# Joining the attention blocks of three chunk pairs on TensorE: Y and S with the next pair's A

## The chip, the cores and the metric

The kernel runs on one core of one Trainium2 chip. The metric is the device time of one execution in microseconds (us); lower is better.

## The reference

Retention with a decaying state, then a feed-forward layer with the activation h * cos(h). Shapes: q, k, v are (4, 8, 768, 64); w_in is 512 x 2048, w_out 2048 x 512; everything is float32.

```python
for t in range(S):                                   # attention, per batch and head
    state = gamma * state + outer(k[t], v[t])
    y[t] = scale * q[t] @ state
h = x @ w_in                                         # x: y as (3072, 512)
out = (h * np.cos(h)) @ w_out
```

## The kernel before

The sequence is cut into chunks of 128 steps. One "pair" p is one chunk of two batches; there are 12 pairs (0 to 11). For each pair TensorE does three small jobs beside the large feed-forward matmuls:

- A: scores, k times q. The contraction is only 64 deep, so two heads run at once in the upper and lower 64 rows of the array (64x128 tiling).
- Y: the outputs, from the masked scores and from the state. Each result is 64 columns wide, so two heads run at once in the left and right half (128x64 tiling).
- S: the update of the state, also in 128x64 tiling.

Each of these jobs writes its results into banks. A bank is one of the program's seven 128x512 PSUM tiles, and it is free again when another engine has read it; the state has a tile of its own. Between A and Y, VectorE masks the scores (`stage_m`). After S it copies the state to SBUF. Y is cast by ScalarE into `xt`, the input of the feed-forward units.

```python
def stage_a(p, b):                       # A: 8 matmuls, row tiling
    ...
    for a in range(HP):
        for j in range(2):
            po = 64 * j
            nc.tensor.matmul(ap[j][:, a, :], lhsT=kt(n, b, a)[po : po + 64, :],
                             rhs=qt(n, b, a)[po : po + 64, :], tile_position=(po, 0))

def half_y(p, b):                        # Y: 16 matmuls, column tiling
    ...
            nc.tensor.matmul(yp[ts(j, 64), a, :], lhsT=stb[p % 2][:, b, a, ts(j, 64)],
                             rhs=qt(n, b, a), start=True, stop=False, ...)
            ...
            nc.tensor.matmul(yp[ts(j, 64), a, :], lhsT=vs[n][:, b, 2 * a + j, :],
                             rhs=am[p % 2][b][j][:, a, :], ...)
    nc.scalar.copy(out=xt[...], in_=yp)

def stage_s(p, copy_st):                 # S: 16 matmuls, column tiling, then the state copy
    ...
                    nc.tensor.matmul(st_ps[ts(j, 64), b, a, :], lhsT=qk[n][:, b, 1, h, :],
                                     rhs=vs[n][:, b, h, :], ...)
    for j in range(2):
        copy_st(out=stb[(p + 1) % 2][...], in_=st_ps[ts(j, 64)])
```

From the third group of pairs on, a loop spreads this over "units". A unit is one feed-forward quarter (`unit_f`, four 128x128 by 128x512 matmuls) and mostly one output quarter (`unit_o`, four more). A of a pair stands at unit 2 of its eight, Y and S (`later`) at unit 6:

```python
for g in range(2, NG + 1):
    for s in range(16):
        hf, r = divmod(s, 8)
        p = 2 * (g + 1) + hf
        ...
            unit_f(g, s)
        ...
                unit_o(g - 1, *divmod(s, 4))
        if p < NP:
            if r == 0:
                ahead(p + 1)             # conversions on GpSimd and ScalarE
            elif r == 1:
                stage_t_dma(p + 1)       # transposes of q and k by DMA
            elif r == 2:
                todo = [stage_a(p, b) for b in range(2)]
                stage_m(p, todo[0])
            elif r == 3:
                stage_m(p, todo[1])
            elif r == 6:
                later(p)                 # Y, S, then the loads of a pair behind
```

Of the kernel before, what the change touches and what calls it, by code (L numbers as in the profile page):

```python
# [47 lines left out]
def kernel(  # L48
# [9 lines left out]
    nc = tc.nc  # L58
    B, H, S, D = q.shape
    C = 128  # L60
    NC = S // C
# [22 lines left out]
    clk = Clock()  # L84
# [42 lines left out]
    def load(eng, p, names):  # L127
        bp, c = divmod(p, NC)
        for n in names:
            t, src = SRC[n[0]]  # L130
            b = int(n[1])
            eng.dma_start(  # L132
                out=t[SLOT[p]][b],
                in_=src[2 * bp + b, :, ds(c * C, C)].rearrange("h t d -> t h d"))
# [65 lines left out]
    def conv_v(p, eng, bs=(0, 1)):  # L200
        for b in bs:
            eng.tensor_tensor(out=vs[p % NB][:, b], in0=vf[SLOT[p]][b],  # L202
                              in1=bc(gk, p % NC), op=ALU.mult)
# [33 lines left out]
    def stage_t_dma(p):  # L237
        n = p % NB
        for b in range(2):
            nc.sync.dma_start_transpose(  # L240
                out=qkt[n][:, b].rearrange("p w a t -> p (w a) t"),
                in_=qk[n][:, b].rearrange("p w h d -> p (w h d)"))
# [7 lines left out]
    def stage_a(p, b):  # L250
        n = p % NB
        bk = [banks.take(), banks.take()]
        ap = [t.rearrange("p (a t) -> p a t", a=HP) for t in bk]
# [4 lines that stand above are left out]
                                 rhs=qt(n, b, a)[po : po + 64, :],  # L258
                                 tile_position=(po, 0))
        clk.run("pe", 0.3)  # L260
        return b, bk, ap, clk.pe

    def stage_m(p, item, parts=(0, 1)):
        b, bk, ap, done = item
        for j in parts:
            nc.vector.tensor_tensor(  # L266
                out=am[p % 2][b][j], in0=ap[j],
                in1=mask.unsqueeze(1).to_broadcast([128, HP, 128]), op=ALU.mult)
            banks.give(bk[j], clk.run("dve", 0.64, done + 0.1))
# [22 lines left out]
    def stage_s(p, copy_st):  # L292
        c = p % NC
        n = p % NB
        if c == NC - 1:
            return
        for b in range(2):
            for a in range(HP):
                for j in range(2):
                    h = 2 * a + j  # L300
                    nc.tensor.matmul(  # L301
                        st_ps[ts(j, 64), b, a, :], lhsT=qk[n][:, b, 1, h, :],
                        rhs=vs[n][:, b, h, :], start=(c == 0 and b == 0 and a == 0),
                        stop=True, skip_group_check=True)
        for j in range(2):
            copy_st(out=stb[(p + 1) % 2][ts(j, 64), :, :, ts(j, 64)], in_=st_ps[ts(j, 64)])  # L306
            clk.run("act" if copy_st == nc.scalar.copy else "dve", 0.65, clk.pe + 0.3)
        clk.run("pe", 0.25)

    def stage_y(p, copy_st=nc.vector.tensor_copy):  # L310
        for b in range(2):
            half_y(p, b)
        stage_s(p, copy_st)
# [15 lines left out]
    def unit_f(g, f):  # L329
        bank = banks.take()  # L330
        for i in range(KIN):
            nc.tensor.matmul(bank, lhsT=w_in_t(i, f), rhs=xt[g % 2][:, i, :],  # L332
                             start=(i == 0), stop=(i == KIN - 1))
        banks.give(bank, act(bank, gt[g % 2][:, f, :]))
# [33 lines left out]
    def unit_o(g, j, part):  # L368
        if part == 0:
            o_bank[j] = banks.take()  # L370
        bank = o_bank[j]
        for f in range(4 * part, 4 * part + 4):
            nc.tensor.matmul(bank, lhsT=gt[g % 2][:, f, ts(j, 128)], rhs=w_out_sb[:, f, :],  # L373
                             start=(f == 0), stop=(f == KOUT - 1))
        clk.run("pe", 0.87)
        if part == 3:
            o = ob[j % 4]
            bp, c = divmod(2 * g + j // 2, NC)
            dst = out[ds((2 * bp + j % 2) * S + c * C, C), :]
            nc.scalar.copy(out=o, in_=bank)  # L380
            nc.sync.dma_start(out=dst, in_=o)
            banks.give(bank, clk.run("act", 0.6, clk.pe + 0.1))

    def last_o(g, j):
        bp, c = divmod(2 * g + j // 2, NC)
        dst = out[ds((2 * bp + j % 2) * S + c * C, C), :]
        for i, (a, n) in enumerate(((0, 320), (320, 192))):
            bank = banks.take()
            for f in range(KOUT):
                nc.tensor.matmul(bank[:, :n], lhsT=gt[g % 2][:, f, ts(j, 128)],  # L390
                                 rhs=w_out_sb[:, f, ds(a, n)],
                                 start=(f == 0), stop=(f == KOUT - 1))
            o = ob[i]
            if i:
                nc.vector.tensor_copy(out=o[:, :n], in_=bank[:, :n])
                nc.scalar.dma_start(out=dst[:, ds(a, n)], in_=o[:, :n])
            else:
                nc.scalar.copy(out=o[:, :n], in_=bank[:, :n])
                nc.sync.dma_start(out=dst[:, ds(a, n)], in_=o[:, :n])
# [61 lines left out]
    clk.run("pe", 0.0, 12.4)  # L461
    stage_m(1, stage_a(1, 1))
    stage_s(0, nc.scalar.copy)
    half_y(0, 1)
    warm(3)
    half_y(1, 0)
    banks.give(spare, clk.pe)
    half_y(1, 1)
    stage_s(1, nc.scalar.copy)
    first_f()  # L470
    for f in range(4, 16):
# [53 lines left out]
    def ahead(p):  # L525
        if p < NP:
            conv_q(p, nc.gpsimd)
            conv_k(p, True)
            conv_v(p, nc.gpsimd)

    def later(p):
        stage_y(p)
        n = 8 if p == 4 else p + 3 if p > 5 else NP
        if n < NP:
            load(nc.gpsimd, n, ("q0", "k0", "q1", "k1", "v0", "v1"))

    def o_units(g, a, b):
        for u in range(a, b):
# [4 lines left out]
    stage_t_dma(6)  # L543
    o_units(1, 2, 6)
    later(4)
    attend(5)
    o_units(1, 6, 10)
    later(5)
# [5 lines that stand above are left out]
            if g == 2 and s % 2 == 0 and s < 12:  # L554
                unit_o(1, *divmod(10 + s // 2, 4))
            if g < NG:
                unit_f(g, s)
            if g > 2:
                if g < NG or s < 12:
                    unit_o(g - 1, *divmod(s, 4))  # L560
                elif s == 12:
                    last_o(g - 1, 3)
            if p < NP:
                if r == 0:
                    ahead(p + 1)
                elif r == 1:
                    if p + 1 < NP:
                        stage_t_dma(p + 1)
                elif r == 2:
                    todo = [stage_a(p, b) for b in range(2)]  # L570
                    stage_m(p, todo[0])
                elif r == 3:
                    stage_m(p, todo[1])
                elif r == 6:
                    later(p)


# [28 lines left out]
```

## Time and profile before

| | before |
|---|---|
| time, median of 6 runs | 209.66 us (209.38 to 210.15) |
| span of the profile | 208.1 us |
| PE busy | 201.2 us, 97% |
| granted TensorE clock (share of full speed) | 0.998 |

The first part of the page gives busy time, share of the span and count of instructions for each engine:

```profile
PE 201.2 (97%) x1646; PEld 113.0 (54%) x1646; DVE 112.8 (54%) x188; ACT 114.3 (55%) x193; POOL 102.3 (49%) x118
```

The chain that ended last, as shares of the span by engine:

```profile
PE 92%; DMA 3%; DVE 2%; issue 1%; SPq 0%; ACT 0%; DVEq 0%
```

The list of waits of PE (engine, line, what it waited for, total us, times, longest):

```profile
PE bank L407 <- DVE gt L172: 1.2, 1, 1.2
PE bank L257 <- DVE qkt L214: 1.1, 2, 0.6
PE bank L230 <- DVE qk L195: 0.9, 1, 0.9
```

The kernel is bound by TensorE, and all three waits lie in the start-up. After it, TensorE waits for no one. A change on another engine can therefore gain nothing after the start-up; only TensorE's own stream can get shorter. Where is that stream not dense? The timeline of PE shows it (columns: start us, duration us, engine, line, operation, out<-in, shapes, count). First the lone A block of pair 9, then the lone Y and S block of the same pair:

```profile
119.95 1.03 PE L373 MATMUL bank<-w_out_sb,gt 128*128 128x512 bf16 x4
120.91 0.62 PE L257 MATMUL bank<-qkt 64*128 64x128 bf16 x16
121.46 1.05 PE L332 MATMUL bank<-xt,w_in 128*128 128x512 bf16 x4
...
127.53 1.03 PE L373 MATMUL bank<-w_out_sb,gt 128*128 128x512 bf16 x4
128.49 0.25 PE L279 MATMUL bank<-qkt,stb 128*64 128x128 bf16 x2
...
129.40 0.42 PE L301 MATMUL st_ps<-vs,qk 128*64 128x64 bf16 x16
129.75 1.05 PE L332 MATMUL bank<-xt,w_in 128*128 128x512 bf16 x4
```

Ends of matmuls are modelled, so read the starts only. In the dense stream a 128x512 matmul starts every 216 ns, so the four from 119.95 use the array until 120.81. A starts at 120.91, 0.10 us late. Its 16 matmuls start in twos, every 56 ns: until 121.36. The next dense one starts at 121.46, again 0.10 us late. It is the same on entering Y (128.39 and 128.49) and on leaving S. In the single records the second step after an edge is longer by another 10 to 28 ns. I call such a change between 128x128, 64x128 and 128x64 an edge; each costs 0.10 to 0.13 us.

Not every change of operands is an edge. The transposes on TensorE in the same trace use other weights, another bank and only 128 columns, but the whole array:

```profile
36.77 1.03 PE L373 MATMUL bank<-w_out_sb,gt 128*128 128x512 bf16 x4
37.63 1.06 PE L230 MATMUL bank<-ident,qk 128*128 128x128 bf16 x16
38.52 0.81 PE L373 MATMUL bank<-w_out_sb,gt 128*128 128x512 bf16 x3
```

Four times 216 ns after 36.77 is 37.63, and 16 times 56 ns later is 38.52: nothing is lost on either side.

The loads of weights show what an edge is made of. These two lines are of PEld, one at an edge, one in the dense stream:

```profile
120.90 0.45 PEld L257 LDWEIGHTS <-qkt 64*128 64x128 bf16 x16 [0.42 <-issue]
...
122.14 0.74 PEld L373 LDWEIGHTS <-gt 128*128 128x128 bf16 x4
122.35 1.03 PE L373 MATMUL bank<-w_out_sb,gt 128*128 128x512 bf16 x4
```

In the dense stream the weights are loaded 0.21 us ahead of their matmul (122.14 for 122.35), during the matmul in front. At the edge they are loaded only when A begins (120.90 for 120.91). The Trainium skill, "TensorE: Matmul & The Clock Gate", Part 2, says that TensorE pulls weight loads ahead of matmuls in flight when the row groups do not conflict or the load goes to the background weight buffer. This trace agrees in the dense stream, where the load leads by 0.21 us; at the edges it leads by 1 to 5 ns only. That the pipeline has to empty there is what the skill's "TensorEngine Tiling (Array Packing)", Key Properties, states; the trace shows the gap, not the emptying itself.

### The profile page before, as it was taken

How to read it: one execution, taken by the hardware profiler on the slowest of the kernel's cores; microseconds unless marked ns; L12 is line 12 of the kernel's file. 1: busy time of each engine (PE TensorE's matmuls, PEld its weight loads, DVE VectorE, ACT ScalarE, POOL GpSimd, SP SyncE). 2: the span in 40 equal slices, each digit the busy share in tenths (PEclk: the TensorE clock that was granted, in tenths of full speed). 3: DMA queues.
4: the chain of work that ended last, by engine and by line, in shares of the span. 5: the costliest groups of instructions: out<-in, count | busy, mean ns of one | idle time of the engine just before them, and what ended most of it. 6: DMA issues, size and time to landing. Idle time of an engine off the chain costs nothing.

```text
span 208.1 us, 4181 instructions
## 1 busy us (share of the span) xinstructions
PE 201.2 (97%) x1646; PEld 113.0 (54%) x1646; DVE 112.8 (54%) x188; ACT 114.3 (55%) x193; POOL 102.3 (49%) x118
## 2 busy tenths in 40 slices
PE   7789999999999999999999999999999999999993
PEld 3257554558897555546545445445445444444452
DVE  4691984544957454869874574574575234443000
ACT  6677873157996336577654744744534653553120
POOL 8999238389999999999999200000000000000000
PEclk9999999999999999999999999999999999999999
DMA  6999999999999999979895231141101101110212
GB/s 161 345 240 200 215 251 290 330 247 306 277 221 276 297 211 303 236 217 225 259 226 193 76 80 49 61 97 50 50 3 50 50 9 45 50 52 16 85 74 81
DMA packets 36644, 33.83 MB, mean 163 GB/s; under 512 B 26768, under 2 KB 29072, under 8 KB 36624
## 3 DMA queue, kind: packets, MB, share of 16 engines
q0 software_dynamic: 7808, 20.98, 37.6%
q1 hardware_dynamic: 28672, 12.49, 24.0%
q8 instruction: 13, 0.21, 0.4%
q10 hardware_dynamic: 144, 0.10, 0.1%
q14 instruction: 7, 0.06, 0.1%
HBM read 27.26 MB, written 6.29 MB: 161 GB/s over the span
## 4 chain that ended last, share of the span: by engine, by line
PE 92%; DMA 3%; DVE 2%; issue 1%; SPq 0%; ACT 0%; DVEq 0%
PE bank L373 38%; PE bank L332 32%; PE bank L343 7%; PE bank L257 3%; DMA qf<-in_q_dram 3%; PE bank L279 3%; PE bank L284 3%; PE bank L390 2%; PE st_ps L301 1%; DVE am L266 1%; PE bank L354 1%; PE bank L230 1%; PE bank L361 1%; DVE qkt L214 1%; SPq L132 0%
## 5 line engine op out<-in xcount | busy, mean ns | idle before, releaser
L325 DVE TENSOR_TENSOR gt<-bank,cosb 128x512 bf16<-128x512 f32 x96 | 64.9, 689 | 63.5 <-ACT cosb L321 63.3
L321 ACT ACTIVATE cosb<-bank,halfpi 128x512 bf16<-128x512 f32 x96 | 65.1, 688 | 50.3 <-PE bank L332 45.9
L373 PE MATMUL bank<-w_out_sb,gt 128*128 128x512 bf16 x368 | 89.6, 379 | 0.0
L332 PE MATMUL bank<-xt,w_in 128*128 128x512 bf16 x304 | 75.4, 380 | 0.0
L373 PEld LDWEIGHTS <-gt 128*128 128x128 bf16 x368 | 35.5, 98 | 41.3
L332 PEld LDWEIGHTS <-w_in 128*128 128x128 bf16 x304 | 33.5, 114 | 30.3
L266 DVE TENSOR_TENSOR am<-bank,mask 128x512 bf16<-128x512 f32 x48 | 30.4, 682 | 1.1 <-PE bank L257 1.1
L380 ACT COPY ob<-bank 128x512 f32<-128x512 f32 x23 | 13.4, 586 | 17.9 <-PE bank L373 17.9
L132 POOL DMA_DIRECT2D vf<-in_v_dram x23 | 20.2, 884 | 5.3 <-DMA w_out_sb<-in_moe_w_out_dram 5.3
L202 POOL TENSOR_TENSOR vs<-vf,gk 128x512 bf16<-128x512 f32 x21 | 21.4, 1040 | 0.4 <-PE st_ps L301 0.3
L195 POOL TENSOR_TENSOR qk<-qf,gq 128x512 bf16<-128x512 f32 x18 | 18.6, 1058 | 2.9 <-DMA qf<-in_q_dram 2.8
L132 POOL DMA_DIRECT2D kf<-in_k_dram x21 | 18.9, 900 | 1.8 <-DMA w_out_sb<-in_moe_w_out_dram 1.6
L208 ACT CAST qk<-kf 128x512 bf16<-128x512 f32 x24 | 13.9, 615 | 9.3 <-DMA kf<-in_k_dram 9.2
L288 ACT CAST xt<-bank 128x512 bf16<-128x512 f32 x24 | 13.0, 587 | 7.9 <-PE bank L284 7.7
L132 POOL DMA_DIRECT2D qf<-in_q_dram x18 | 16.2, 901 | 0.8 <-DMA w_in<-in_moe_w_in_dram 0.8
L343 PE MATMUL bank<-xt,w_in 128*128 128x256 bf16 x128 | 14.7, 273 | 0.0
L343 PEld LDWEIGHTS <-w_in 128*128 128x128 bf16 x128 | 13.8, 114 | 0.4
L284 PE MATMUL bank<-am,vs 128*64 128x128 bf16 x192 | 11.7, 220 | 0.0
L279 PEld LDWEIGHTS <-stb 128*64 128x64 bf16 x160 | 8.8, 109 | 4.3 <-issue 3.1
L306 DVE CAST stb<-st_ps 64x512 bf16<-64x512 f32 x12 | 8.2, 687 | 4.9 <-PE st_ps L301 4.7
L279 PE MATMUL bank<-qkt,stb 128*64 128x128 bf16 x160 | 10.7, 222 | 0.1
L284 PEld LDWEIGHTS <-vs 128*64 128x64 bf16 x192 | 10.0, 110 | 0.5 <-issue 0.4
(46 smaller groups left out, 86.2 us busy)
## 6 DMA issues: line engine op xcount, KB each, us to landing
vf<-in_v_dram POOLq DMA_DIRECT2D x23, 256.0 KB, 5.9
out_dram<-ob SPq DMA_DIRECT2D x23, 256.0 KB, 2.0
kf<-in_k_dram POOLq DMA_DIRECT2D x21, 256.0 KB, 5.9
qf<-in_q_dram POOLq DMA_DIRECT2D x18, 256.0 KB, 5.6
w_out_sb<-in_moe_w_out_dram POOLq DMA_DIRECT2D x4, 512.0 KB, 12.9
qf<-in_q_dram SPq DMA_DIRECT2D x6, 256.0 KB, 7.8
w_in<-in_moe_w_in_dram POOLq DMA_DIRECT2D x3, 512.0 KB, 8.1
kf<-in_k_dram POOLq DMA_DIRECT2D x1, 512.0 KB, 6.1
```

The source lines that it names most:

```text
L132: eng.dma_start(out=t[SLOT[p]][b], in_=src[2 * bp + b, :, ds(c * C, C)].rearrange("h t d -> t h d"))
L195: eng.tensor_tensor(out=qk[p % NB][:, b, 0], in0=qf[SLOT[p]][b], in1=bc(gq, p % NC), op=ALU.mult)
L202: eng.tensor_tensor(out=vs[p % NB][:, b], in0=vf[SLOT[p]][b], in1=bc(gk, p % NC), op=ALU.mult)
L208: nc.scalar.copy(out=qk[p % NB][:, b, 1], in_=kf[SLOT[p]][b])
L266: nc.vector.tensor_tensor(out=am[p % 2][b][j], in0=ap[j], in1=mask.unsqueeze(1).to_broadcast([128, HP, 128]), op=ALU.mult)
L279: nc.tensor.matmul(yp[ts(j, 64), a, :], lhsT=stb[p % 2][:, b, a, ts(j, 64)], rhs=qt(n, b, a), start=True, stop=False, skip_group_check=True)
L284: nc.tensor.matmul(yp[ts(j, 64), a, :], lhsT=vs[n][:, b, 2 * a + j, :], rhs=am[p % 2][b][j][:, a, :], start=(c == 0), stop=True, skip_grou ...
L321: nc.scalar.activation(out=cb, in_=bank, func=AF.Sin, bias=halfpi)
L325: nc.vector.tensor_tensor(out=out, in0=bank, in1=cb, op=ALU.mult)
L332: nc.tensor.matmul(bank, lhsT=w_in_t(i, f), rhs=xt[g % 2][:, i, :], start=(i == 0), stop=(i == KIN - 1))
L343: nc.tensor.matmul(bank[:, ts(e, 256)], lhsT=w_in_t(i, f + e), rhs=xt[g % 2][:, i, ts(hf, 256)], start=(i == 0 and e == 0), stop=(i == KIN ...
L373: nc.tensor.matmul(bank, lhsT=gt[g % 2][:, f, ts(j, 128)], rhs=w_out_sb[:, f, :], start=(f == 0), stop=(f == KOUT - 1))
```

## The change

Y and S of pairs 8, 9 and 10 are placed in the same block as A of the pair behind (9, 10, 11). Two lone blocks have four edges (in and out of each); a joined one has three (in, S to A, out). To let A follow S directly, the state copy of S is put off by two units, behind the masks. The last pair's loads stand two units sooner in the program. Its core:

```diff
+    def state_out(p, copy_st):            # the state copy, taken out of stage_s
+        ...
+    joined = {(3, 10): 8, (3, 14): 9, (4, 10): 10}
+
+    def join(p, now):
+        stage_y(p, None)
+        todo = [stage_a(p + 1, b) for b in range(2)]
+        stage_m(p + 1, todo[0])
+        put_off(now + 1, lambda: stage_m(p + 1, todo[1]))
+        put_off(now + 2, lambda: state_out(p, nc.vector.tensor_copy))
 ...
-                elif r == 2:
+                elif r == 2 and p in (6, 7, 8):
                     todo = [stage_a(p, b) for b in range(2)]
 ...
-                elif r == 6:
+                elif r == 6 and p in (6, 7, 11):
                     later(p)
+                elif (g, s) == (3, 4):
+                    fetch(11)
+                if (g, s) in joined:
+                    join(joined[g, s], 16 * g + s)
```

More of the change, by code (lines that the diff above doesn't have):

```diff
@@ L304, in stage_s @@
                         stop=True, skip_group_check=True)
+        clk.run("pe", 0.25)
+        if copy_st is not None:
+            state_out(p, copy_st)
+    def state_out(p, copy_st):
+        if p % NC == NC - 1:
+            return
         for j in range(2):
             copy_st(out=stb[(p + 1) % 2][ts(j, 64), :, :, ts(j, 64)], in_=st_ps[ts(j, 64)])
-            clk.run("act" if copy_st == nc.scalar.copy else "dve", 0.65, clk.pe + 0.3)
-        clk.run("pe", 0.25)
+            clk.run("act" if copy_st == nc.scalar.copy else "dve", 0.65, clk.pe + 0.1)
     def stage_y(p, copy_st=nc.vector.tensor_copy):
@@ L529, in ahead, with fetch @@
             conv_v(p, nc.gpsimd)
+    def fetch(p):
+        load(nc.gpsimd, p, ("q0", "k0", "q1", "k1", "v0", "v1"))
     def later(p):
@@ L534, in later, with put_off @@
         if n < NP:
-            load(nc.gpsimd, n, ("q0", "k0", "q1", "k1", "v0", "v1"))
+            fetch(n)
+    late = []
+    def put_off(when, step):
+        late.append((when, step))
+    joined = {(3, 10): 8, (3, 14): 9, (4, 10): 10}
[5 more added lines that the diff above has]
+        put_off(now + 2, lambda: state_out(p, nc.vector.tensor_copy))
     def o_units(g, a, b):
@@ L562 @@
                     last_o(g - 1, 3)
+            while late and late[0][0] <= 16 * g + s:
+                late.pop(0)[1]()
             if p < NP:
@@ L568 @@
                         stage_t_dma(p + 1)
-                elif r == 2:
+                elif r == 2 and p in (6, 7, 8):
                     todo = [stage_a(p, b) for b in range(2)]
                     stage_m(p, todo[0])
-                elif r == 3:
-                    stage_m(p, todo[1])
-                elif r == 6:
+                    put_off(16 * g + s + 1, lambda todo=todo, p=p: stage_m(p, todo[1]))
+                elif r == 6 and p in (6, 7, 11):
                     later(p)
+                elif (g, s) == (3, 4):
+                    fetch(11)
+                if (g, s) in joined:
+                    join(joined[g, s], 16 * g + s)
 _INS = ['q', 'k', 'v', 'moe_w_in', 'moe_w_out']
```

## The prediction

> **What bounds the kernel now.** TensorE. The page has PE busy 97% of the 208.1 us span, and the chain of waits puts 92% of the span on PE. The list of waits shows only three PE waits over the run, all in the start-up, and none after 20 us: From there on the 128x512 matmuls start every 216 ns. What is not dense is the edges of the attention blocks. Reading single start times (timeline of PE and PEld around 120.6 and 128.2 us):
>
> - last dense matmul to first of A: 311 ns for 216, then 63 for 56: about 105 ns for entering A;
> - last of A to first dense: 149 ns for about 53, then 242 for 216: about 122 ns for leaving;
> - entering Y: 309 for 216, then 76 for 56: about 115 ns; leaving S: 128 for about 29, then 242 for 216: about 125 ns.
>
> The Trainium skill, "TensorEngine Tiling (Array Packing)", Key Properties, says that changing the tiling mode drains the TensorE. These gaps agree: dense is 128x128, A is 64x128, Y and S are 128x64.
>
> **What the change removes, adds and moves.** TensorE's instructions are the same in number; only the order differs. For pairs 8, 9 and 10 the Y/S block and the A block of the next pair become one, so there is one edge fewer each time: leaving S (125) and entering A (105) are gone, and a direct S-to-A edge is added. The kernel before already has such a joined block once, at 70.4 to 72.7 us: S to A there is 128 ns for 29, then 62 for 56, about 105 ns. So one join saves about 125 ns. From sums: a lone Y/S block costs 1.387 us over dense matmuls, a lone A block 0.675; the joined one 1.94. Three joins: about 0.37 us.
>
> The state copy moves two units later on VectorE (2 x 0.70 us), behind the first-half and second-half masks (2 x 0.64 us each). The earlier loads change nothing: the order of instructions on GpSimd, SyncE is the same in both kernels, and GpSimd runs ahead of TensorE (done at 116 us).
>
> **On the critical path.** All of the 0.37 us, if no new wait arises. Candidates, estimated from the trace's durations:
> - one of A's banks belongs to the feed-forward unit just before. Its multiply ends 2.5 us after that unit begins; A's second half begins 3.4 us after.
> - Y of the next pair, four units (some 7 us) after the join, needs masks and state: done about 1 us before.
> - pair 10's transposes are issued at 118 to 120.6 us and land in 2.7 to 7.6 us; A now needs them at about 130.
>
> **Predicted time.** 209.74 - 0.37 = 209.37 us; the runs differ by 0.4 among themselves. Range 208.95 to 209.95. Faster by over 2%: 0.01; within 2%: 0.98; slower by over 2%: 0.01.
>
> **What would show it right or wrong.** Right: span near 207.7 us; lone groups near 113, 137 and 144 us gone, joined ones near 121, 129 and 153 with S to A in 128 ns; no PE wait in the list of waits after 20 us; other starts keep 216 ns. VectorE's state copies at about 2 units after S, its total unchanged.
>
> **What would make it wrong.** A PE wait on VectorE in a join (bank still held by a multiply or mask), or on the transposes of pair 10; each could cost 0.3 to 1 us and turn the gain into a small loss.

## The result, and the profile after

| | before | after | after, in later rounds |
|---|---|---|---|
| median time, us | 209.66 (6 runs) | 209.60 (6 runs) | 209.27 (6 runs; before 209.76) |
| ratio to before | | 0.9994 (0.9977 to 1.0011) | 0.9972 (0.9953 to 0.9991) |
| span of the profile, us | 208.1 | 207.8 | 207.3 |
| stretch, us | 137.848 | 137.473 | 137.475 |

A ratio is the mean time of one kernel's fast runs over that of the other's of the same rounds, so it is not quite the ratio of the medians. The bracket is its 95% interval.

By the total time of the first rounds one could not say that anything was gained: the same program gave 0.9994 once and 0.9972 another time. The stretch says it clearly. It runs from the start of the first matmul of A of pair 4 (near 66 us) to the start of the last matmul of the run, read from single records, and it leaves out the start-up. It became 0.375 us shorter. The changed kernel, profiled twice, repeats it within 0.002 us. The kernel before has one profile, but two experiments with as many edges read within 0.007 us of it.

The page's first part after the change, and the list of waits of PE after it:

```profile
PE 200.2 (96%) x1646; PEld 112.9 (54%) x1646; DVE 113.3 (55%) x188; ACT 114.3 (55%) x193; POOL 102.2 (49%) x118
```

```profile
PE bank L230 <- ACT qk L208: 1.5, 1, 1.5
PE bank L413 <- DVE gt L172: 1.2, 1, 1.2
PE bank L257 <- DVE qkt L214: 1.1, 2, 0.6
```

TensorE has the same 1646 matmuls, and all of its waits are still in the start-up. The timeline of PE at the first join, Y and S of pair 8 with A of pair 9:

```profile
118.63 1.03 PE L379 MATMUL bank<-w_out_sb,gt 128*128 128x512 bf16 x4
119.59 0.25 PE L279 MATMUL bank<-qkt,stb 128*64 128x128 bf16 x2
...
120.50 0.42 PE L301 MATMUL st_ps<-vs,qk 128*64 128x64 bf16 x16
120.85 0.62 PE L257 MATMUL bank<-qkt 64*128 64x128 bf16 x16
121.41 1.05 PE L338 MATMUL bank<-xt,w_in 128*128 128x512 bf16 x4
```

S leads into A with the same 0.35 us that led it into the dense stream before (129.40 to 129.75), and A leads out as before. In single records S to A takes 127 to 128 ns in all three joins, as predicted. The entry into A and the slow second matmul after S are gone. That is one edge.

Why does the total hide it? The start-up scatters. Here is the first long wait in the chain of waits of three profiles (start us, us, what): of the kernel before, of the changed kernel, and of the experiment with six joins, which has the same program up to there:

```profile
1.88 6.03 DMA qf<-in_q_dram
```

```profile
1.26 5.03 DMA kf<-in_k_dram
```

```profile
4.18 5.99 DMA kf<-in_k_dram
```

The chain hangs on another of the first loads, or on the same at another time, in each. Over all 13 profiles the first matmul of A of pair 4 starts between 65.73 and 66.65 us, 0.9 us apart, more than twice the gain. Nearly all of it arises before the first matmul of A of pair 1, near 12 us: from there to A of pair 4 twelve profiles take 53.68 to 53.69 us (that of e3_split 53.90, which was not explained). Seven of the profiles (that of the kernel before among them) hang on the load of `qf` from 1.88 us on. It takes 5.53 to 6.12 us in them, and in each of the seven A of pair 1 starts 6.84 or 6.85 us plus this time into the span, at 12.37 to 12.97 us: there the scatter is that of the load. In the two profiles compared here the changed kernel reached A of pair 4 0.076 us later than the kernel before, so that 0.298 us of the 0.375 were left in the span.

### The profile page after: what moved, and what is told of

Same layout as the page of the kernel before. It is cut to its first block, busy times and chain, and to the rows that moved or that the text cites. A ratio compares the mean times of both kernels' runs of the same rounds, so it can differ in the third digit from the quotient of the medians.

```text
span 207.8 us, 4176 instructions
## 1 busy us (share of the span) xinstructions
PE 200.2 (96%) x1646; PEld 112.9 (54%) x1646; DVE 113.3 (55%) x188; ACT 114.3 (55%) x193; POOL 102.2 (49%) x118
## 4 chain that ended last, share of the span: by engine, by line
PE 92%; DVE 3%; DMA 2%; issue 1%; ACT 1%; SPq 0%; DVEq 0%
PE bank L379 39%; PE bank L338 32%; PE bank L349 7%; PE bank L257 3%; PE bank L279 3%; PE bank L284 3%; DMA kf<-in_k_dram 2%; PE bank L396 2%; PE st_ps L301 1%; DVE am L266 1%; PE bank L230 1%; PE bank L360 1%; PE bank L367 1%; DVE qkt L214 1%; DVE qk L195 1%
```

## The experiments

Theory: each edge costs about 0.1 us, the gain is one edge for each join, and nothing else in the change matters. Rivals: the late state copy or the early loads made the gain; or it is the number of interruptions of the wide matmuls, not of tiling changes, that counts; or the order of work is made up for elsewhere.

| run | edges against before | stretch, us | minus before, us | median time, us | ratio to before |
|---|---|---|---|---|---|
| before | 0 | 137.848 | | 209.66 | |
| after | -3 | 137.473 | -0.375 | 209.60 | 0.9994 |
| e1_late_only | 0 | 137.844 | -0.004 | 209.90 | 1.0013 |
| e2_join_now | -3 | 137.472 | -0.376 | 209.20 | 0.9984 |
| e3_split | +24 | 140.662 | +2.814 | 212.47 | 1.0136 |
| e5_seam | 0 | 137.971 | +0.123 | 209.77 | 1.0016 |
| e6_sandwich | 0 | 137.841 | -0.007 | 210.01 | 1.0014 |
| e4_join6 | -4 | 139.448 | +1.600 | 211.30 | 1.0091 |
| e9_five | -5 | 137.488 | -0.360 | 209.11 | 0.9973 |
| e10_five_swap | -5 | 137.233 | -0.615 | 209.08 | 0.9969 |
| e8_six | -6 | 137.366 | -0.482 | 211.52 | 1.0044 |
| e11_six_swap | -6 | 138.448 | +0.600 | 212.23 | 1.0015 |

The last two medians contain slow runs, the ratios do not. All results were correct. In all cuts of code and edits, remarks after # are mine.

One rival fell without a run, by a build alone. The changed kernel was built once with the last pair's loads back at their old place; the instructions of all five engines and the waits between them came out identical. GpSimd meets the same instructions in the same order either way.

### No join, only the late state copy and the early loads

```diff
-                elif r == 2 and p in (6, 7, 8):
+                elif r == 2:
 ...
+                elif r == 6:                       # pairs 8, 9, 10
+                    stage_y(p, None)
+                    put_off(16 * g + s + 2, lambda p=p: state_out(p, nc.vector.tensor_copy))
-                if (g, s) in joined:
-                    join(joined[g, s], 16 * g + s)
```

> No block is joined; only the state copies of pairs 8, 9 and 10 come two units later and the last pair's loads stand two units sooner. I read the stretch from the first matmul of A of pair 4 to the last matmul of the run: 137.85 us before, 137.47 us after the change. Edge theory (each change of tiling mode on TensorE costs about 0.1 us, and one join saves one): 137.85, within 0.03, as no edge is gone. Rival theory (the gain comes from VectorE's later state copies, which free banks sooner, or from the earlier loads): 137.47.

The stretch was 137.844 us, that of before. So the late copy and the loads gain nothing by themselves.

### The joins, with the state copy at once

```diff
-        stage_y(p, None)
+        stage_y(p)
 ...
-        put_off(now + 2, lambda: state_out(p, nc.vector.tensor_copy))
```

> The three joins stay, but the state copy follows S at once, ahead of the masks. Edge theory: the stretch stays at 137.47 us, within 0.03, with no PE wait after 20 us; VectorE has some us to spare. Rival theory (the late state copy is what makes the join possible): PE waits for VectorE's masks appear, 0.3 us or more a join, and the stretch comes to 138.3 or more.

The stretch was 137.472 us, as after the change, and no wait came. So the late state copy is not needed for these three joins either. The joins alone make the gain.

### The opposite dose: every half in a block of its own

From the kernel before, pairs 6 to 11:

```diff
-                    todo = [stage_a(p, b) for b in range(2)]
-                    stage_m(p, todo[0])
+                    stage_m(p, stage_a(p, 0))
                 elif r == 3:
-                    stage_m(p, todo[1])
+                    stage_m(p, stage_a(p, 1))
+                elif r == 5:
+                    half_y(p, 0)
                 elif r == 6:                       # then half_y(p, 1) and S
```

> From the kernel before, with the opposite dose: for pairs 6 to 11 the two halves of A stand in two units, and the two halves of Y too, so twelve more blocks, each with one more entering and one more leaving. Edge theory: 6 x 0.227 + 6 x 0.240 = 2.8 us more, the stretch 140.65 us (within 0.25), the time about 212.4 us, ratio 1.013. Rival theory (TensorE has the same work, and the gaps are hidden or made up elsewhere): stretch at 137.85, ratio 1.000.

Twelve more blocks, so 24 more edges, made the stretch 2.81 us longer: 0.117 us an edge, and the total ratio 1.0136 (1.0122 to 1.0150) now stands clear of the scatter. The same work in another order is not made up for elsewhere. In the timeline of PE each half block now pays both of its edges:

```profile
104.76 0.81 PE L373 MATMUL bank<-w_out_sb,gt 128*128 128x512 bf16 x3
105.50 0.40 PE L257 MATMUL bank<-qkt 64*128 64x128 bf16 x8
105.83 1.05 PE L332 MATMUL bank<-xt,w_in 128*128 128x512 bf16 x4
106.72 1.03 PE L373 MATMUL bank<-w_out_sb,gt 128*128 128x512 bf16 x4
107.68 0.40 PE L257 MATMUL bank<-qkt 64*128 64x128 bf16 x8
```

Eight matmuls of A need 0.22 us, but take 0.33 from 105.50 to 105.83, after an entry 0.10 late.

### One full-array matmul in the seam

```diff
+        if seam:                                   # before A's own matmuls, once in each join
+            nc.tensor.matmul(ap[0][:, 0, :], lhsT=kt(n, b, 0), rhs=qt(n, b, 0),
+                             start=True, stop=True, skip_group_check=True)
```

> The changed kernel with one full-array 128x128 matmul (56 ns; its result is overwritten by A) in the seam between S and A of each join. Edge theory: the seam then has two changes of mode where it had one, so each join loses its 0.123 us and pays 0.056 for the matmul: the stretch is 137.47 + 3 x 0.18 = 138.01 us (within 0.05), slower than the kernel before. Rival theory (what costs is leaving the long run of 512-column matmuls and coming back, not the mode): only the matmul itself is added, 137.47 + 3 x 0.056 = 137.64.

The stretch was 137.971 us, 0.166 us a join more than after the change, of which the matmul itself is 0.056. The timeline of PE:

```profile
119.90 0.42 PE L304 MATMUL st_ps<-vs,qk 128*64 128x64 bf16 x16
120.25 0.23 PE L255 MATMUL bank<-qkt 128*128 128x128 bf16 x1
120.41 0.62 PE L260 MATMUL bank<-qkt 64*128 64x128 bf16 x16
```

A single short matmul of the whole array, with no wide matmuls near it, brings back the edge: 120.25 to 120.41 is 0.16 us for one of 56 ns. This matmul writes the same bank as A's first, but the 0.107 us that are lost behind it are about what is lost on entering A from the wide matmuls (0.096), where no bank is shared.

### A between the halves of Y

```diff
-        stage_y(p, None)
+        half_y(p, 0)
         todo = [stage_a(p + 1, b) for b in range(2)]
+        half_y(p, 1)
+        stage_s(p, None)
```

> In each join A stands between the two halves of Y: first half of Y, A, second half of Y, S. It is still one block in the run of wide matmuls, but has four changes of mode, as many as the two lone blocks of the kernel before; the changed kernel has three. Edge theory: the whole gain is gone, the stretch (first matmul of A of pair 4 to the last matmul of the run) is 137.85 us, within 0.05. Rival theory (it is the number of interruptions of the wide matmuls that counts): 137.47, as after the change.

The stretch was 137.841 us. One block with as many edges as two gains nothing over two. In the single records both inner edges show: from Y to A 152 ns and from A to Y 145 ns, where 53 is the step within either. Together with the seam this settles it for this kernel: what counts is changes of tiling, not interruptions.

### A fourth join at a tight place

```diff
-    joined = {(3, 10): 8, (3, 14): 9, (4, 10): 10}
+    joined = {(2, 10): 6, (3, 10): 8, (3, 14): 9, (4, 10): 10}
```

(with A of pair 7 taken out of its lone place, and the loads of pair 9 left at unit 6)

> A fourth join, Y and S of pair 6 with A of pair 7 at unit 10 of the second-group loop, where units without an output quarter take only 0.87 us and Y of pair 7 follows four units later. Edge theory without waits: 137.35 us for the stretch. My estimate from durations: between this A and Y of pair 7 VectorE has two masks, two multiplies, two masks, state copy (about 5.3 us) in about 3.6 us of TensorE work, so TensorE waits 1 to 2 us near 97 us, and the stretch is 138.4 to 139.3.

The stretch was 139.448 us, 0.15 us above the top of my estimate. The list of waits of PE in this run has a new first line, and the timeline of VectorE shows why:

```profile
PE bank L279 <- DVE stb L313: 1.8, 2, 1.3
```

```profile
95.91 1.28 DVE L266 TENSOR_TENSOR am<-bank,mask 128x512 bf16<-128x512 f32 x2
97.11 0.68 DVE L331 TENSOR_TENSOR gt<-bank,cosb 128x512 bf16<-128x512 f32 x1
97.70 1.40 DVE L313 CAST stb<-st_ps 64x512 bf16<-64x512 f32 x2
```

Y of pair 7 needs the state copy that ends at 99.10. In this part of the loop the units are half as long, and VectorE has no time for masks and copy between two Y blocks. By the starts the late state cost more than the 1.8 us of the list: the stretch is 1.975 us over that after the change, where a fourth join should have saved 0.12. An edge saved is worth 0.12 us, a late state here 2.1.

### Five joins

```diff
-    joined = {(3, 10): 8, (3, 14): 9, (4, 10): 10}
+    joined = {(2, 6): 6, (3, 10): 8, (3, 14): 9, (4, 10): 10}
 ...
     o_units(1, 6, 10)
-    later(5)
+    join(5, 32)
```

> Five joins: those of the change, and Y of pair 5 with A of pair 6, Y and S of pair 6 with A of pair 7 four units sooner than in the run with four joins, where VectorE has time. A's transposes have landed by then (pair 6 about 75 us, pair 7 about 86 us in the trace of before). Edge theory without waits: 137.47 - 2 x 0.123 = 137.23 us for the stretch. Rival (the banks or VectorE are too tight while the units are short): a PE wait between 77 and 95 us, stretch above 137.47.

The stretch was 137.488 us instead of 137.23, so the rival named in the expectation, banks that are too tight, came true. The join of pairs 5 and 6 worked as expected; in that of pairs 6 and 7, A's 16 matmuls stood still for 0.26 us in the middle. Lines of the timeline of this run:

```profile
86.82 0.69 ACT L327 ACTIVATE cosb<-bank,halfpi 128x512 bf16<-128x512 f32 x1 [1.04 <-PE bank L338]
87.41 1.06 ACT L288 CAST xt<-bank 128x512 bf16<-128x512 f32 x2
87.54 0.88 PE L257 MATMUL bank<-qkt 64*128 64x128 bf16 x16
88.34 0.58 PEld L338 LDWEIGHTS <-w_in 128*128 128x128 bf16 x4
```

The matmul that stood still writes the bank that the first half of Y had used, and the program lets it wait for ScalarE's cast of that half. By single records that cast ended at 87.99 us and the matmul followed at 88.04. The cast was late because ScalarE first had the activation of the feed-forward quarter issued just before Y.

### Five joins, with the quarters swapped

At unit 6 of that group the output quarter is issued after the feed-forward quarter instead of before it.

> Five joins as in the run with five, whose stretch was 137.488 us and whose join at 87 us stood 0.26 us longer inside A; I read that as A's third bank being that of the feed-forward unit issued just before. Here the output quarter of that unit is issued after the feed-forward unit instead of before it, so 0.86 us of TensorE work lies between. If that reading is right: no gap inside A, the stretch is 137.23 us (within 0.03), and the total 0.62 us under the kernel before (ratio 0.9970). If the gap has another cause: 137.49 again.

The stretch was 137.233 us, and the stop inside A was gone. The expectation names the wrong bank: it put the stop down to the bank of the feed-forward quarter, while the records of the run before point to the bank of Y's first half. The swap lets ScalarE finish the activation earlier, so it helps in both readings and does not tell them apart. The program does: built again, the run with five writes that quarter to bank 4 and Y's first half to bank 1, and A takes banks 0, 2, 5 and 1. By the stretch this version beats both kernels. By the total it beats the kernel before (median 209.08 us, ratio 0.9969, 0.9940 to 0.9998), but cannot be told from the changed kernel of the same rounds (0.9972).

### Six joins, without and with the swap

Y and S of pair 7 with A of pair 8 as well (`(2, 14): 7`).

> Six joins: as the five, and Y and S of pair 7 with A of pair 8 at the end of that group. Edge theory without waits: 137.47 - 3 x 0.123 = 137.10 us for the stretch, total time 0.75 us under the kernel before (ratio 0.9964). Risk: the second half of pair 8's transposes lands between 97 and 101 us in the trace of before, and A of pair 8 would start at about 98.6: then a PE wait of up to 2 us on that transfer, and the stretch is 137.5 to 139.

> Six joins with the same swap. Without waits the stretch is 137.10 us. The run with six joins had times from 208.59 to 216.52 us; I put the spread down to A of pair 8 waiting for its transposes in some executions. If so: the total again spreads by more than 1 us above 209, and a profile of a slow one shows a PE wait near 98 us. If the spread was chance of that job: 208.9 with a spread of 0.5.

The first gave 137.366 us in its profile (the same 0.26 us stop inside A as with five), but times from 208.59 to 216.52 us, and from 208.59 to 211.62 in its fast runs alone. The second gave 138.448 us, 1.35 more than it should have without waits, and its profile caught a wait of the kind that I had named. A line of its list of waits of PE, and the block of A of pair 8 in its timeline of PE:

```profile
PE bank L257 <- DMA qkt<-qk: 1.2, 1, 1.2
```

```profile
98.14 0.40 PE L257 MATMUL bank<-qkt 64*128 64x128 bf16 x8
99.71 0.40 PE L257 MATMUL bank<-qkt 64*128 64x128 bf16 x8 [1.17 <-DMA qkt<-qk]
```

The second half of A waits for the transposed q and k of pair 8; by the starts it stands 1.33 us, which is the whole loss of this profile. In the profile of the first kernel they were there in time. This suggests that the join depends on a transfer that comes now sooner, now later, but the two kernels also differ by the swap. Fast runs of the second kernel lie between 209.51 and 210.92 us; that the wait makes the spread of either kernel was not shown, as each run has one profile. Three of its six runs and two of the other's are slow, at a granted clock of 0.982 to 0.992. Why those fall so often on these two kernels stays open.

### The changed kernel again

> The changed kernel itself, in the same rounds, as a control of the total time: the stretch 137.47 us again within 0.01; the total 0.37 us under the kernel before (ratio 0.9982), with an interval that is likely to hold 1, as the start-up before 66 us scatters by some 0.6 us.

The stretch was 137.475 us, as expected. The ratio was 0.9972, and its interval (0.9953 to 0.9991) does not hold 1, against what I thought likely.

## Why the prediction was right

The predicted 209.37 us lay within the measured runs (209.08 to 209.87; median 209.60), and the range held it. That alone says little: a kernel that gained nothing, at 209.66, would have lain in the range too. What bears the prediction out is the stretch and the experiments. Point by point:

- **Bound by TensorE, with edges as the loss that can be removed.** Right, after the start-up. The run with edges added and the runs with edges kept all follow the count of edges, at 0.12 us each; the runs with more joins do where no wait came.
- **0.125 us a join, 0.37 us in all.** Right: 0.375 us in the stretch. The estimate came from a joined block that the kernel before already had, so even the seam had been measured.
- **The loads change nothing.** Right, since the program is identical with them moved back. But GpSimd did not stay done at 116 us. Its last conversion now waits for the later S of pair 8, and ends at 122.98. The timeline of GpSimd after the change:

```profile
120.94 2.04 POOL L202 TENSOR_TENSOR vs<-vf,gk 128x512 bf16<-128x512 f32 x2 [3.09 <-PE st_ps L301]
```

  Y of the last pair, which reads the result, starts only at 159.94, so it costs nothing. The prediction missed this wait.
- **No new wait on TensorE.** Right. Y of pair 9 needs the state copy, the third of these lines of VectorE's timeline after the change:

```profile
123.83 1.28 DVE L266 TENSOR_TENSOR am<-bank,mask 128x512 bf16<-128x512 f32 x2
125.02 0.68 DVE L331 TENSOR_TENSOR gt<-bank,cosb 128x512 bf16<-128x512 f32 x1
125.62 1.40 DVE L313 CAST stb<-st_ps 64x512 bf16<-64x512 f32 x2
```

  It ends at 127.02, Y starts at 128.43: 1.4 us to spare, against the 1 us predicted.
- **A wait could cost 0.3 to 1 us.** Waits like those named could be brought about by joining more: 0.26 us for a bank (held by a cast on ScalarE, where the prediction named VectorE), 1.3 us for transposes, and 2.1 us for the state. The last two are more than was said.
- **The total.** The expected difference of 0.37 us showed as 0.06 us in the medians of the first rounds and 0.49 us in the later ones. The prediction saw 0.4 us of scatter among the runs, but not where it comes from: the start-up, and the first loads in it.

## What to carry to other kernels

Count how often TensorE changes its tiling in a run of small matmuls, and group work of one tiling together; here each change costs about 0.12 us, however little work lies between two of them. Before moving a block, check the engine that has to finish between it and its consumer: a wait on it can cost more than ten times the edge (2.1 us for a late state here). When a gain is smaller than the scatter of the start-up, compare a stretch of the trace that begins after it.

## What the Trainium skill lacked or had wrong

- "TensorEngine Tiling (Array Packing)", Key Properties, says that a change of tiling mode drains TensorE, but gives no cost. Here a change costs 0.09 to 0.10 us in the first start and 0.01 to 0.03 in the second; per edge 0.117 us in the run with 24 edges added, 0.125 in the joins.
- "TensorE: Matmul & The Clock Gate", Back-to-back issue gap, gives sustained figures of about 81 ns for N=128 and about 131 ns for N=512 in streams of weight load and matmul. Here such streams start every 56 ns (the transposes at 37.6 us) and every 216 ns, which are the figures that the page calls isolated.
- The same page, Part 2, describes weight loads pulled ahead of matmuls; it does not say that this stops at a change of tiling. Here the load leads by 0.21 us in the dense stream and by 0.001 to 0.005 us at an edge.
